# A sliding-window attention block with a token-mixing MLP on one Trainium2 core: a new head, a new order of the attention stage, and a rearranged tail

## The chip, the core and the metric

The kernel runs on one core of a Trainium2 chip. The core has five engines that run side by side and meet through semaphores: TensorE (PE, matmuls; its weight loads are shown apart as PEld), VectorE (DVE), ScalarE (ACT), GpSimd (POOL) and SyncE (SP), which here only issues DMA transfers. The metric is the device time of one execution in microseconds (us). Before the change three runs took 251.11 us (median; 250.66 to 253.0).

## The reference

`x` is 2048 tokens by 512 channels. A condition vector `c` gives six modulation rows. Then come two residual branches: attention with 32 heads of 16 channels in a causal window of 256 tokens, and an MLP that mixes tokens (its matrices act along the token axis).

```python
mod = (silu(c) @ w_mod).reshape(1, 6, 1, 512)        # sa, ca, ga, sb, cb, gb
h = layernorm(x) * (1 + ca) + sa
q, k, v = heads(h @ wqkv)
p = softmax(where(0 <= i - j < 256, q k^T / 4, -1e9))
x = x + ga * ((p v) @ wo)
h = layernorm(layernorm(x) * (1 + cb) + sb)          # the MLP has a layernorm of its own
u = gelu(h^T @ w1 + b1)                              # w1: 2048 x 1792
x = x + gb * (u @ w2 + b2)^T                         # w2: 1792 x 2048
```

## The kernel before

**Tiles.** Tokens lie in 16 tiles of 128 (`xres[t]`), in four groups of four. Heads lie in groups of eight (128 channels), so that "slice" `s` (0 to 15) is group of tokens `s // 4` and group of heads `s % 4`.

**Head** (L498 to L627, written out by hand). The four first tiles of `x`, the modulation columns for `sa` and `ca` (`wmod`, v = 0 and 1, one DMA each, L339) and `wqkv` are loaded. TensorE runs "fills", `warm(n)`, L504: matmuls on zeros whose result nobody reads. Two small matmuls (L521) spread the seeds of the window's masks, which ScalarE copies to `mask_k` and `mask_q`. `fm(v)` (L546) makes the modulation as columns with 16 one-column matmuls. `norm_x(tl)` (L570) normalises a tile on VectorE, after a reciprocal root that GpSimd takes (`rstd_of`, L438); `turn_x(tl)` (L577) transposes it on TensorE, `modulate` (L598) scales and shifts the transposed rows into `h1T[0]` on VectorE and ScalarE. TensorE's order is: fills 2, c's transpose, fills 8, mask seeds, fill 1, `fm(0)`, fills 2, tiles 0 and 2, fill 1, `fm(1)`, tiles 1 and 3, fills 2. Eight dense steps (L613) then project K and Q of slice 0 into two banks, four (L617) the Q of slice 1 ("second"). Q is padded with zeros for even and odd heads (`QP`, L620, three pieces on VectorE), K is evicted by ScalarE (L624), second by VectorE to `QR[1]` (L626). ScalarE also writes the ones in V (`ones_of`).

**Attention stage** (L630 to L1182). The work is cut into tasks: 76 score units `S0` to `S75` (four for slices 0 to 3, five for each later one), each with two exponentials `E` of 128 x 1024 on ScalarE; two products `P{s}.{par}` per slice; dense groups on TensorE (`Kk`, `Qq`, `V`, `Wo` of four steps, `B` of eight steps), where a step is one 128 x 512 matmul or its four 128 x 32 quarters, with an eviction each; transposes of normalised tiles (`T`); `turn`, `recip` and `back` on VectorE with `merge` on GpSimd for the softmax division; layer norm tasks (`st1`, `ap1`, `s2`, `p2`, `m2`, `s3`, `p3`); DMA tasks on SP (`L.`, `VLU`, `bc`, `w1.`). A unit of kind A or B writes scores with 12 or 4 matmuls and then adds the masks with 8 or 12 (L716, L706, L724); kind C has 32 and 8 (L688, L697). Scores go to `ps_s`, three buffers of two banks; a unit takes two. Everything else on TensorE shares two banks, `bk0` and `bk1`.

At build time a planner (`Order`, L128) lays these tasks into one fixed order per engine. Ranks come from the table `PLACE`, earliest starts from `START`, and `PATIENCE` says how long a score unit may be held back. `HEAD_PE` only tells the planner how many TensorE instructions the head has. `BY_POOL` lists the blocks whose second layer norm is applied by GpSimd alone. `B4` to `B13` are the MLP's first matrix over the first eight token tiles, for the ten columns blocks in `PART`; they are evicted to `part` (L1177), and can fill TensorE early.

TensorE's planned order in the places that matter (x4 is four steps):

```
S0 V0.3x4 V0.0x2 S1 V0.0x2 V0.1x2 S2 V0.1x2 V0.2x4 S3 Kk3x4 Kk1x4 Kk2x4 S4 Qq2x4 P0.0 S5 P0.1 Qq3x2 S6 ...
... S40 Wo4x4 Wo7x2 S41 Wo7x2 P8.1 S42 ...
... S74 B11x4 B4x2 S75 B4x6 P15.0 P15.1 B10x8 B13x8
```

**Tail** (L1201 on). The score buffers are released to `pu0` (four banks) and `pu1` (two), in which the MLP's first matmul collects its first six column blocks; `ps_big` (two buffers for `pa`) takes the banks `bk0` and `bk1`. `t_wo(tb)` (L1252) projects the attention output of blocks 12 to 15, `t1`, `t2`, `t3` (L1273 to L1284) are their two layer norms on VectorE with the root on GpSimd; the last result is `hb[12..15]`, applied by `t_apply` (L1268). `emit_b1_group0_sc(sc)` (L1229) is a mixing step: the matmuls of token tile `sc` into `pu0` and `pu1`, four of them for `sc` below 8 and six above. `load_rest` (L1210) starts the loads of the rest of `w1` (`w1b`) and of `w2` once block 12 is projected. Then follow the remaining columns with gelu (L1318, L1245) and the second matrix (L1344) with the output.

```python
for step in range(6):
    if step < 4:
        done = t_wo(12 + step)
        if step:
            emit_b1_group0_sc(step - 1)
        else:
            load_rest(done)
    for f, n in ((t1, step), (t2, step - 1), (t3, step - 2)):
        if 0 <= n < 4:
            f(12 + n)
for sc in range(3, NT):
    emit_b1_group0_sc(sc)
```

Of the kernel before, what the change touches and what calls it, by code (L numbers as in the profile page):

```python
# [27 lines left out]
V0.3 0 V0.0 1 V0.1 2 V0.2 3 T1.1 4 Kk3 5 V1.3 6 P1.1 7 Kk4 8 P2.0 9 P1.0 10 Qq4 11 Kk1 12 mods 13 Kk2 14 Wo0 15 Wo1  # L28
16 P4.0 17 P2.1 18 V1.0 19 Qq8 20 V1.2 21 Qq5 22 Kk6 23 P5.0 24 P3.1 25 V1.1 26 Qq2 27 Qq6 28 T2.0 29 P0.0 30 T1.0
31 P0.1 32 Qq3 33 P3.0 34 P8.1 35 Kk8 36 Wo4 37 Kk5 38 bias 39 P5.1 40 V2.0 41 P4.1 42 Wo3 43 Qq7 44 Wo2 45 T2.1 46  # L30
V2.2 47 P6.1 48 P6.0 49 Kk7 50 Kk15 51 Qq12 52 T3.1 53 T3.0 54 P9.1 55 Wo7 56 P9.0 57 P8.0 58 Wo6 59 V3.3 60 Qq9 61
V2.1 62 V2.3 63 Kk10 64 P7.1 65 P7.0 66 Wo5 67 Kk11 68 V3.0 69 P10.1 70 P10.0 71 V3.2 72 P11.0 73 B12 74 Qq13 75
V3.1 76 Kk12 77 B7 78 Kk13 79 P13.1 80 Kk14 81 P12.0 81 P11.1 82 P14.0 83 P13.0 84 B5 85 B6 86 Wo9 87 Qq15 88 Wo11
89 P12.1 90 Wo10 91 Qq14 92 P14.1 93 P15.1 94 B8 95 B9 96 B11 97 B4 98 Wo8 99 P15.0 100 B10 101 B13 102 Qq11 103
Qq10 104 Kk9 105 Wo0. 0 turn4.1 1 Qq4. 2 recip0 3 turn2.0 4 Wo1. 5 st1.1.2 6 Qq3. 7 Kk7. 8 st1.2.1 9 V2.2. 10
turn0.1 11 recip1 12 Kk2. 13 Qq7. 14 p2.2 15 mods. 16 V3.3. 17 recip3 18 T1.1. 19 Kk11. 20 V0.2. 21 recip5 22 back1
23 Kk4. 24 turn3.1 25 V1.3. 26 turn5.1 26 V2.0. 27 s2.3 28 turn1.0 29 back9 30 Kk1. 31 B12. 32 turn1.1 33 T1.0. 34
recip4 35 recip9 36 Wo2. 37 back0 38 Kk8. 39 back5 40 V1.0. 41 p2.4 42 Kk10. 43 Kk6. 44 Qq6. 45 p2.1 46 Qq12. 47
recip7 48 Kk3. 49 turn7.1 50 bias. 51 turn5.0 52 Wo3. 53 turn7.0 54 turn6.1 55 turn0.0 56 V1.1. 57 T2.1. 58 Qq2. 59
s2.1 60 Qq5. 61 V1.2. 62 V2.1. 63 s3.1 64 turn2.1 65 back2 66 V0.1. 67 back6 68 st1.1.1 69 back3 70 turn3.0 70  # L40
st1.1.3 71 st1.2.2 72 recip2 73 s3.0 74 st1.3.3 75 T2.0. 76 turn9.0 77 s2.2 78 Qq8. 79 Kk15. 80 st1.2.0 81 V0.3. 82
T3.0. 83 fold3 84 Kk5. 85 back4 86 st1.2.3 87 turn9.1 88 st1.1.0 89 Wo6. 90 fold0 91 fold2 92 fold1 93 Qq10. 94
V0.0. 95 s3.2 96 recip6 97 s2.0 98 turn6.0 99 turn4.0 100 st1.3.1 101 st1.3.0 102 back8 103 Wo5. 104 Wo7. 105 Wo4.
106 V2.3. 107 s2.6 108 s2.7 109 Kk9. 110 back7 111 T3.1. 112 s2.5 113 turn8.1 114 Qq11. 115 recip8 116 s3.3 117
turn8.0 118 s2.4 119 Qq9. 120 st1.3.2 121 Qq13. 122 s3.8 123 V3.2. 124 s3.10 125 turn14.0 126 s3.11 127 B5. 128 B6.
129 back12 130 turn15.1 131 B11. 132 recip15 133 turn13.0 134 Wo9. 135 back14 136 s2.9 137 s3.9 138 B10. 139 V3.0.
140 turn14.1 141 B13. 142 back11 143 turn12.1 144 recip14 145 turn10.1 146 recip13 147 turn15.0 148 Kk13. 149 B8.
150 turn11.1 151 Kk14. 152 turn12.0 153 s3.5 154 B7. 155 p2.6 156 p2.7 157 B4. 158 s3.4 159 V3.1. 160 recip11 161
Kk12. 162 turn10.0 163 turn13.1 164 Qq15. 165 s2.11 166 recip10 167 s2.8 168 turn11.0 169 Wo10. 170 s3.7 171 Wo11.
172 p2.9 173 recip12 174 s3.6 175 Wo8. 176 s2.10 177 back10 178 Qq14. 179 p2.11 180 back15 181 B9. 182 back13 183  # L50
r1.1 0 zeros 1 Qp4.1 2 ap1.1.2 3 Qp3.1 4 VLU0a 5 m2.0 6 q2.0 7 p2.0 8 ap1.1.3 9 merge3 10 Qp8.1 11 ap1.3.2 12 r1.2
13 Qp11.1 14 ones2 15 VLU0 16 ap1.1.0 17 Qp5.0 18 Qp7.0 19 r1.3 20 Qp1.1 21 Qp4.0 22 Qp1.0 23 Qp2.1 24 m2.2 24 p3.2
25 Qp10.0 26 merge6 27 ap1.2.0 28 Qp5.1 29 Qp12.0 30 ap1.3.1 31 ap1.3.3 32 m2.3 33 m2.1 34 ap1.2.3 35 p3.0 36 merge1
37 ap1.2.1 38 merge9 39 merge2 40 Qp3.0 41 ap1.1.1 42 Qp2.0 43 merge0 44 Qp9.0 45 Qp6.0 46 merge4 47 Qp8.0 48
ap1.3.0 49 Qp7.1 50 Qp6.1 51 ap1.2.2 52 ones1 53 Qp11.0 54 merge5 55 p3.5 56 merge8 57 Qp10.1 58 m2.4 59 p3.3 60
Qp9.1 61 merge7 62 p2.3 63 merge11 64 Qp13.0 65 merge10 66 p2.5 67 p3.8 68 q3.2 69 merge15 70 p3.9 71 p3.10 72
merge14 73 m2.5 74 m2.7 75 q2.2 76 Qp14.1 77 m2.9 78 merge13 79 p3.7 80 Qp13.1 81 m2.6 82 Qp15.1 83 p3.6 84 p2.8 85
q2.1 86 merge12 87 m2.8 88 p3.1 89 p3.11 90 m2.10 91 q3.1 92 p2.10 93 p3.4 94 Qp12.1 95 q3.0 96 Qp15.0 97 Qp14.0 98
m2.11 99 w1.7 0 VLU8 1 VLU11 2 w1.11 3 VLU14 4 VLU5 5 bc. 6 w1.10 7 L.x14 8 VLU3 9 w1.0 10 VLU13 11 w1.2 12 w1.12 13
VLU10 14 L.wo1 15 w1.5 16 w1.13 17 VLU4 18 w1.4 19 L.m2.1 20 L.m4.1 20 w1.8 21 VLU15 22 bc1 23 w1.3 24 VLU12 25 L.x8  # L60
26 L.x11 27 L.x12 28 w1.15 29 VLU2 30 L.m5.1 31 L.m4.0 32 L.m5.0 33 L.m3.1 34 VLU1 35 w1.9 36 VLU9 37 w1.14 38
L.m2.0 39 bc3 40 L.x15 41 VLU7 42 w1.6 43 L.x13 44 VLU6 45 L.x9 46 L.m3.0 47 bc0 48 bc2 49 w1.1 50 L.b1 51 L.x10 52
# [60 lines left out]
HEAD_PE = 148  # L123
# [141 lines left out]
def kernel(  # L265
# [72 lines left out]
    for v in (0, 1):  # L338
        dma.dma_start(out=wmod[:, :, v * D : (v + 1) * D], in_=w_mod_v[:, :, v * D : (v + 1) * D])  # L339
# [84 lines left out]
    def ones_of(n, a):  # L424

        nc.scalar.activation(
            out=Vring[n][:, 2 * a : 2 * a + 2, :, DH : 2 * DH],
            in_=zero[:].rearrange("p (a h d) -> p a h d", a=2, d=DH), func=ACT.Identity, scale=0.0, bias=1.0,
        )

# [7 lines left out]
    def rstd_of(var, n, name):  # L438
        ve = small.tile([P, n], DT.float32, name=name + "_ve")
        nc.gpsimd.tensor_scalar(out=ve[:], in0=var, scalar1=EPS, scalar2=0.0, op0=ALU.add, op1=ALU.add)  # L440
        r = small.tile([P, n], DT.float32, name=name)
        nc.gpsimd.tensor_tensor(out=r[:], in0=ve[:], in1=mhalf[:, 0:n], op=ALU.pow)
        return r
# [54 lines left out]
    with tc.manual_schedule():  # L498
# [19 lines left out]
        warm(8)  # L518
        rows = bank(1)
        for n in range(2):  # L520
            nc.tensor.matmul(rows[:, 0:NS], lhsT=spread[n][:], rhs=seed[n][:], start=n == 0, stop=n == 1)  # L521
# [12 lines left out]
        for odd in range(2):  # L534
            r1[0, odd] = rstd_of(mv1[0][:, odd : odd + 3 : 2, 1], 2, "r1")
        nc.scalar.activation(out=mask_k[:], in_=rows[:, 0:192], func=ACT.Copy)
        for n, c0 in ((0, MF), (1, MO)):
            nc.scalar.activation(
                out=mask_q[:, 128 * n : 128 * n + 128].rearrange("p (a b) -> p a b", a=2),
                in_=rows[:, c0 : c0 + 64].unsqueeze(1).to_broadcast([P, 2, 64]), func=ACT.Copy,  # L540
            )
        for a in range(2):
            ones_of(0, a)
        ps_fm = ps_s.tile([P, 8], DT.float32, name="pss")

        def fm(v):  # L546
            for oc in range(ND):
                col = v * ND + oc
                for k in range(ND):
# [27 lines left out]
        def turn_x(tl):  # L577
            for dc in range(ND):
                nc.tensor.transpose(place(dc, tl, tl + 1), xn1[0, tl][:, dc * P : (dc + 1) * P], identity[:])
# [37 lines left out]
        for dc in range(4):  # L617
            dense_step(second[:], wqkv[:, dc, P : 2 * P], h1T[0][:, dc, :], dc == 0, dc == 3)
# [770 lines left out]
```

## Time and profile before

| what | value |
|---|---|
| three runs | 251.11 us median (250.66, 251.11, 253.0) |
| the profiled execution | 251.63 us, of which the span from first to last instruction is 249.9 |
| TensorE busy | 240.5 us (96%) |
| VectorE, ScalarE, GpSimd busy | 168.1, 157.7, 125.2 us |
| the 152 exponentials | 140.6 us busy |
| DMA | 28.14 MB, mean 113 GB/s |

A group of the page reads: line, engine, operation, tile written and tiles read, shapes, count; then busy time, mean ns of one, and the idle time of the engine just before them with what ended it. The chain that ended last is printed as start, length, what; the timeline as start, length, engine, line, operation, and in brackets the idle time before. Matmuls overlap, so the length of a row of n matmuls is longer than n times their distance by the last one's own duration. A wait row names who waited for whom, the total, the times and the longest.

### The profile page before, as it was taken

Reading aid. Unit: us, or ns where it says so; the run is one execution under the profiler, and the core shown is the slowest. Engines: PE = TensorE matmul, PEld = TensorE weight load, DVE = VectorE, ACT = ScalarE, POOL = GpSimd, SP = SyncE. Lnnn points to the kernel's source line nnn. Section 1 sums busy time; section 2 is a strip of 40 time slices with the busy share of each in tenths; the row PEclk is TensorE's granted clock in tenths of the full one; section 3 lists DMA queues with packets and bytes.
Section 4 is the critical chain, followed back from the end, with each engine's and each line's share of the span. In section 5 each row is a group of like instructions: output and inputs, shape, how many; then the busy total and the mean of one; then the engine's idle time right before and its main releaser. Section 6 shows DMA issues by size and latency. Waiting matters only on the chain.

```text
span 249.9 us, 10602 instructions
## 1 busy us (share of the span) xinstructions
PE 240.5 (96%) x4710; PEld 126.5 (51%) x4710; DVE 168.1 (67%) x324; ACT 157.7 (63%) x183; POOL 125.2 (50%) x228
## 2 busy tenths in 40 slices
PE   8999999989999999999999999989999999999994
PEld 2644745545654555655554664544444444444443
DVE  7686879869997978787958686679824404251544
ACT  5467999999999999999999999200056300000000
POOL 5536952980299999869894997724400000000000
PEclk9999999999999999999999999999999999999999
DMA  6935554332460444211201010059999000201121
GB/s 202 325 106 152 149 140 137 108 76 77 121 201 3 97 121 114 74 34 23 42 10 37 18 22 3 3 164 390 415 410 384 6 0 5 81 28 56 42 88 42
DMA packets 25490, 28.14 MB, mean 113 GB/s; under 512 B 10212, under 2 KB 22628, under 8 KB 25444
## 3 DMA queue, kind: packets, MB, share of 16 engines
q1 hardware_dynamic: 25148, 27.20, 34.8%
q8 instruction: 37, 0.61, 1.0%
q10 hardware_dynamic: 296, 0.26, 0.3%
q14 instruction: 9, 0.07, 0.1%
HBM read 22.03 MB, written 2.10 MB: 97 GB/s over the span
## 4 chain that ended last, share of the span: by engine, by line
PE 72%; ACT 14%; DVE 5%; POOL 3%; DMA 3%; issue 2%; SPq 0%; ACTq 0%; POOLq 0%
PE py L1344 19%; ACT et L734 13%; PE bk L473 11%; PE bk L477 8%; PE pu L1234 7%; PE bk L759 6%; PE pu L1318 6%; PE pss L716 5%; PE bk L504 3%; PE pss L688 2%; PE pss L724 2%; PE pa L1255 1%; DMA VU<-V 1%; DMA x<-in_A_x_dram 1%; PE pss L697 1%
## 5 line engine op out<-in xcount | busy, mean ns | idle before, releaser
L734 ACT ACTIVATE et<-pss 128x1024 bf16<-128x1024 f32 x152 | 140.6, 1062 | 3.4 <-PE pss L724 3.3
L1344 PE MATMUL py<-guT,w2r 128*128 128x512 bf16 (+1 forms) x238 | 48.5, 367 | 0.0
L1344 PEld LDWEIGHTS <-w2r 128*128 128x128 bf16 x238 | 23.2, 98 | 25.4
L1351 DVE SCALAR_TENSOR_TENSOR o<-py,bFM,bc_gb 128x512 bf16<-128x512 f32 (+1 forms) x17 | 11.7, 717 | 30.5 <-PE py L1344 30.5
L781 POOL TENSOR_TENSOR merge<-t,zr 128x512 bf16<-128x512 f32 x16 | 17.4, 1084 | 19.4 <-DVE zr L777 19.4
L768 DVE STREAM_TRANSPOSE t<-bk 128x512 f32<-128x512 f32 x32 | 22.6, 710 | 6.6 <-PE bk L759 5.4
L716 PE MATMUL pss<-QP,KT 32*128 32x192 bf16 (+2 forms) x672 | 25.6, 236 | 0.9 <-ACT et L734 0.5
L913 POOL TENSOR_SCALAR QP<-QR,mask_par 128x512 bf16<-128x512 bf16 x30 | 21.6, 724 | 7.7 <-DVE QR L626 4.7
L716 PEld LDWEIGHTS <-KT 32*128 32x128 bf16 x672 | 13.4, 92 | 18.2 <-issue 14.0
L473 PE MATMUL bk<-h1T,wqkv 128*128 128x512 bf16 x76 | 20.4, 382 | 0.3 <-ACT h1T L602 0.3
L759 PE MATMUL bk<-et,V 128*32 128x64 bf16 (+2 forms) x704 | 19.3, 240 | 0.4 <-DVE V L933 0.3
L759 PEld LDWEIGHTS <-V 128*32 128x32 bf16 x704 | 14.7, 96 | 7.8 <-issue 4.2
L724 PE MATMUL pss<-mask_q,mask_k 32*128 32x64 bf16 (+2 forms) x496 | 18.3, 213 | 0.0
L1245 ACT ACT_TABLE_LOAD x1 | 1.3, 1283 | 26.0 <-issue 26.0
L1243 DVE TENSOR_TENSOR gelu_a<-pu,part 128x512 f32<-128x512 f32 x10 | 6.5, 687 | 11.5 <-PE pu L1318 8.7
L1124 POOL TENSOR_TENSOR h<-h,bc_sb 128x512 bf16<-128x512 bf16 x12 | 13.9, 1155 | 0.6
L1318 PE MATMUL pu<-hb,w1b 128*128 128x512 bf16 x64 | 14.0, 379 | 0.0
L724 PEld LDWEIGHTS <-mask_k 32*128 32x128 bf16 x496 | 13.3, 93 | 0.4
L933 DVE CAST V<-bk 128x512 bf16<-128x512 f32 x16 | 11.1, 691 | 3.5 <-PE bk L477 1.5
L477 PE MATMUL bk<-h1T,wqkv 128*32 128x512 bf16 x192 | 12.7, 382 | 0.0
L759 PE MATMUL bk<-et,VU 128*32 128x64 bf16 x448 | 11.8, 194 | 0.9 <-DMA VU<-V 0.9
L759 PE MATMUL bk<-et,VL 128*32 128x64 bf16 x512 | 12.2, 193 | 0.0
(138 smaller groups left out, 406.0 us busy)
## 6 DMA issues: line engine op xcount, KB each, us to landing
w2r<-in_B_w_dram SPq DMA_DIRECT2D x14, 512.0 KB, 10.2
w1a<-in_B_w_dram SPq DMA_DIRECT2D x16, 224.0 KB, 3.2
w1b<-in_B_w_dram SPq DMA_DIRECT2D x8, 448.0 KB, 7.2
wmod<-in_w_mod_dram SPq DMA_DIRECT2D x8, 256.0 KB, 3.0
out_dram<-otile SPq DMA_DIRECT2D x15, 128.0 KB, 1.7
x<-in_A_x_dram SPq DMA_DIRECT2D x14, 128.0 KB, 3.1
VL<-V SPq DMA_DIRECT2D x15, 96.0 KB, 2.8
VU<-V SPq DMA_DIRECT2D x27, 48.0 KB, 2.4
```

Of the source, the lines that this page charges most:

```text
L473: nc.tensor.matmul(out, lhsT=lhsT, rhs=rhs, start=start, stop=stop, skip_group_check=True)
L477: nc.tensor.matmul(out[cols, :], lhsT=lhsT[:, cols], rhs=rhs, start=start, stop=stop, tile_position=(0, 32 * j), skip_group_check=True,)
L716: mm(pss[j // 2][:, j % 2, c0 : c0 + nq], lhsT=keys(4 * tg + kb)[rows[j], :], rhs=QP[s][rows[j], par, q0 : q0 + nq], start=n == 0, stop=False,
L724: mm(pss[j // 2][:, j % 2, c0 : c0 + hi - lo], lhsT=mask_k[rows[j], 0:P], rhs=mask_q[rows[j], lo:hi], start=False, stop=n + 1 == len(masks ...
L734: e = nc.scalar.activation(out=et[:], in_=held.pop(("pss", u, a))[:], func=ACT.Exp, scale=SCORE_SCALE)
L759: nc.tensor.matmul(po[32 * j : 32 * j + 32, q0 : q0 + nq], lhsT=v(j), rhs=held["et", s, k, j // 2][:, j % 2, c0 : c0 + nq], start=n == 0, ...
L768: nc.vector.transpose(out=held["t2", s][:, par, :], in_=psum.pop(("po", s, par))[:])
L781: nc.gpsimd.tensor_tensor(out=m[:].rearrange("p (b a d) -> p a b d", a=2, d=DH), in0=t2v(s, 0, DH, DH), in1=held["zr", s][:].to_broadcast( ...
L913: nc.gpsimd.tensor_scalar(out=QP[s][:, par, :], in0=QR[s][:], scalar1=mask_par[:, par : par + 1], scalar2=0.0, op0=ALU.mult, op1=ALU.add,)
L1234: nc.tensor.matmul(pu[:, i, :], lhsT=w1_of(sc, fc), rhs=hb[sc][:], start=(sc == s0), stop=(sc == NT - 1),)
L1318: nc.tensor.matmul(pu[:, i, :], lhsT=w1_of(sc, fc), rhs=hb[sc][:], start=(sc == s0), stop=(sc == NT - 1),)
L1344: nc.tensor.matmul(pys[4 if lo else tl][:, lo:hi], lhsT=w2r[:, fc, tb * P : (tb + 1) * P], rhs=guT[fc][:, lo:hi], start=(fc == 0), stop=(f ...
```

## The change

The head, the order of the attention stage and the tail are changed; the computation is the same.

- Fills: 2, c's transpose, 10, `fm(0)`, mask seeds, tile 0, half of `fm(1)`, tile 2, the other half, tiles 1 and 3, fills 3. No fill stands from the ten to the last transposes. `fm` runs over k outermost; the DMA of v = 1 is cut in two halves by k, so three `wmod` issues stand ahead of `wqkv` on SP.
- The epsilon of the odd tiles' root is added by VectorE instead of GpSimd.
- The ones in the first V ring are one memset on GpSimd, behind two other memsets, instead of two ScalarE instructions.
- K of slice 0 is evicted in two pieces, columns 128 to 512 first.
- The masks of unit 0 are written ahead of its scores, right behind the eight dense steps; then come two steps of the second projection, unit 0's scores (12 matmuls), and the other two steps with the eviction to `QR[1]`.
- `PLACE`, `START`, `PATIENCE` (236.867 to 399.279), `HEAD_PE` (148 to 158) and `BY_POOL` (0, 3, 5, 8, 10 to 0, 2, 5, 10) are new, and so is each engine's order. Five dense groups of four steps more are issued as quarters. On TensorE:

```
S0 Kk1x4 S1 V0.1x4 V0.0 S2 V0.0x3 Qq2x3 S3 Qq2 V0.2x4 S4 V0.3x4 Kk2x2 S5 Kk2x2 Kk3x4 P0.0 Qq3x4 P0.1 S6 T1.0 T1.1 S7 ...
... S40 Wo4x4 P8.0 S41 Wo5x4 P8.1 S42 ...
... S73 B7x5 S74 B7x3 B13x3 S75 B13x5 P15.0 P15.1 B6x8
```

  On SP, before: `... bc1 L.x12 L.x14 bc3 L.x15 L.x13 bc0 VLU4 VLU5 bc2 w1.0 ...` (bc0 is the four DMAs of `bc_cb`), now `... bc1 L.x12 bc2 L.x14 bc3 VLU4 VLU5 L.x13 bc0 L.x15 VLU6 w1.0 ...`. On GpSimd, at the end, before: `... merge14 m2.10 q3.2 p3.8 p3.9 p3.10 merge15 p3.11`, now `... m2.11 merge14 q3.2 p3.9 p3.11 p3.10 merge15 p3.8`.
- Tail: two mixing steps stand ahead of the first of the last projections. The last apply of blocks 12 to 14 is done by ScalarE, with a shift that GpSimd makes in two small operations.

```diff
-    for v in (0, 1):
-        dma.dma_start(out=wmod[:, :, v * D : (v + 1) * D], in_=w_mod_v[:, :, v * D : (v + 1) * D])
+    for v, ks in ((0, slice(0, ND)), (1, slice(0, 2)), (1, slice(2, ND))):
+        dma.dma_start(out=wmod[:, ks, v * D : (v + 1) * D], in_=w_mod_v[:, ks, v * D : (v + 1) * D])
...
-        warm(8)
-        rows = bank(1)
...
+        warm(10)
...
-        for odd in range(2):
-            r1[0, odd] = rstd_of(mv1[0][:, odd : odd + 3 : 2, 1], 2, "r1")
+        for odd, eng in enumerate((nc.gpsimd, nc.vector)):
+            r1[0, odd] = rstd_of(mv1[0][:, odd : odd + 3 : 2, 1], 2, "r1", eng)
...
-        warm(1)
         for tl in (0, 2):
             norm_x(tl)
-        fm(0)
-        warm(2)
+        fm(0, 0, ND)
+        rows = bank(1)
...
         turn_x(0)
+        fm(1, 0, 2)
         turn_x(2)
         norm_x(1)
         xn_at = norm_x(3)
-        warm(1)
-        fm(1)
+        fm(1, 2, ND)
+        nc.vector.tensor_scalar_add(out=modFM[:, 4:8], in0=ps_fm[:, 4:8], scalar1=1.0)
         turn_x(1)
         turn_x(3)
-        warm(2)
+        warm(3)
...
+        nc.gpsimd.memset(Vring[0][:, :, :, DH : 2 * DH], 1.0)
...
-        nc.scalar.activation(out=Kring[0][:, 0, :], in_=first[1][:], func=ACT.Copy)
+        for lo, hi in ((P, 4 * P), (0, P)):
+            nc.scalar.activation(out=Kring[0][:, 0, lo:hi], in_=first[1][:, lo:hi], func=ACT.Copy)
...
+            second_steps((2, 3))
+            QR[1] = qrpool.tile([P, 4 * P], DT.bfloat16, name="QR")
+            nc.vector.tensor_copy(out=QR[1][:], in_=second[:])
...
+        add_masks([held["pss", 0, 0], held["pss", 0, 1]], MASKS["1"], True)
+        second_steps((0, 1))
...
+        def by_scalar(key):
+            return key[0] == 3 and key[1] < NT - 1
...
         def t_apply(out, src, key):
+            if by_scalar(key):
+                nc.scalar.activation(
+                    out=out, in_=src, func=ACT.Identity, bias=v[key, "shift"][:], scale=v[key, "r"][:],
+                )
+                return
...
+        for sc in range(2):
+            emit_b1_group0_sc(sc)
         for step in range(6):
             if step < 4:
                 done = t_wo(12 + step)
                 if step:
-                    emit_b1_group0_sc(step - 1)
+                    emit_b1_group0_sc(step + 1)
...
-        for sc in range(3, NT):
+        for sc in range(5, NT):
             emit_b1_group0_sc(sc)
```

More of the change, by code (lines that the diff above doesn't have):

```diff
@@ L33 @@
[L33 to L37, printed above, removed]
@@ L58 @@
[L58 to L62, printed above, removed]
@@ L71 @@
+BY_POOL = (0, 2, 5, 10)
 TUNABLE = ()
@@ L422 @@
     nc.gpsimd.memset(add_one[0:32, :], 1.0)
[L424 to L429, printed above, removed]
     ps_s = tc.alloc_tile_pool(name="ps_s", bufs=3, space=PSUM)
@@ L533, with fm @@
         stats_of(xres[3][:], mv1[0][:, 3, :])
-        for odd in range(2):
-            r1[0, odd] = rstd_of(mv1[0][:, odd : odd + 3 : 2, 1], 2, "r1")
[L536 to L543, printed above, removed]
+        for odd, eng in enumerate((nc.gpsimd, nc.vector)):
+            r1[0, odd] = rstd_of(mv1[0][:, odd : odd + 3 : 2, 1], 2, "r1", eng)
         ps_fm = ps_s.tile([P, 8], DT.float32, name="pss")
[L546 to L549, printed above, removed]
+        def fm(v, k0, k1):
+            for k in range(k0, k1):
+                for oc in range(ND):
+                    col = v * ND + oc
                     nc.tensor.matmul(
@@ L616, with second_steps @@
         second = ps_s.tile([P, 4 * P], DT.float32, name="pss")
-        for dc in range(4):
-            dense_step(second[:], wqkv[:, dc, P : 2 * P], h1T[0][:, dc, :], dc == 0, dc == 3)
+        def second_steps(steps):
+            for dc in steps:
+                dense_step(second[:], wqkv[:, dc, P : 2 * P], h1T[0][:, dc, :], dc == 0, dc == 3)
         for par, lo, hi in ((0, 192, 512), (1, 0, 512), (0, 0, 192)):
@@ L638 @@
         slots["qr"].take(1)
-        order.free["DVE"] = 1.6
+        order.free["DVE"] = 1.85
         held, psum = {}, {}
@@ L666, with add_masks @@
         }
+        def add_masks(pss, masks, first):
+            for n, ((lo, hi), c0) in enumerate(masks):
+                for j in range(4):
+                    nc.tensor.matmul(
+                        pss[j // 2][:, j % 2, c0 : c0 + hi - lo], lhsT=mask_k[rows[j], 0:P],
+                        rhs=mask_q[rows[j], lo:hi], start=first and n == 0, stop=not first and n + 1 == len(masks),
+                        tile_position=(32 * j, 0), skip_group_check=True,
+                    )
         def scores(u):
@@ L670, in scores @@
             tg, g8 = divmod(s, 4)
-            pss = [ps_s.tile([P, 2, 4 * P], DT.float32, name="pss") for a in range(2)]
+            pss = [held.get(("pss", u, a)) or ps_s.tile([P, 2, 4 * P], DT.float32, name="pss") for a in range(2)]
             held["pss", u, 0], held["pss", u, 1] = pss
@@ L721, in scores @@
                 masks = MASKS[k[2]]
[L722 to L728 removed]
+            if u:
+                add_masks(pss, masks, False)
+                return
+            second_steps((2, 3))
+            QR[1] = qrpool.tile([P, 4 * P], DT.bfloat16, name="QR")
+            nc.vector.tensor_copy(out=QR[1][:], in_=second[:])
+        held["pss", 0, 0], held["pss", 0, 1] = (ps_s.tile([P, 2, 4 * P], DT.float32, name="pss") for a in range(2))
+        add_masks([held["pss", 0, 0], held["pss", 0, 1]], MASKS["1"], True)
+        second_steps((0, 1))
         def exps(u, a):
```

119 lines of the change are left out of this document (64 added, 55 removed).

## The prediction, on record before the result

> **What bounds the kernel now.** I read the page's head and groups first, then the windows by stage, then the chain that ended last, ScalarE's timeline, and the waits.
>
> ```profile
> span 249.9 us, 10602 instructions
> PE 240.5 (96%) x4710; PEld 126.5 (51%) x4710; DVE 168.1 (67%) x324; ACT 157.7 (63%) x183; POOL 125.2 (50%) x228
> L734 ACT ACTIVATE et<-pss 128x1024 bf16<-128x1024 f32 x152 | 140.6, 1062 | 3.4 <-PE pss L724 3.3
> ```
> ```profile
> 14.90:60.00 45.10, 43.37 (x1223) 24.22 (x1225) 37.66 (x64) 42.69 (x46) 29.16 (x50) 1.00 0.44 116
> 60.00:100.00 40.00, 38.61 (x1188) 22.31 (x1187) 34.57 (x58) 39.96 (x45) 31.57 (x55) 1.00 0.40 110
> 100.00:157.00 57.00, 56.49 (x1646) 31.53 (x1636) 42.81 (x67) 56.99 (x63) 46.51 (x77) 1.00 0.13 29
> ```
>
> A window's columns are its length, then the busy time of TensorE, its weight loads, VectorE, ScalarE, GpSimd. TensorE bounds the whole: what it does before useful work, and every wait, is paid at the end. From the first exponential (14.90) to 157 ScalarE is full too; TensorE's waits there are 1.73 + 1.39 + 0.51 = 3.6 us. After 157 TensorE alone sets the pace.
>
> ```profile
> 20.32 0.33 PE pss L716 x12
> 20.76 2.82 PE bk L477 x48
> ```
> ```profile
> 24.02 0.98 PE bk L477 x16
> 25.00 0.50 PE bk L759 x40
> 25.51 0.33 PE pss L716 x12
> ```
> ```profile
> 56.26 1.40 PE bk L473 x6
> 57.66 0.33 PE pss L716 x12
> ```
> ```profile
> 133.16 0.36 PE pss L688 x32
> 133.52 0.29 PE pss L697 x8
> ```
> ```profile
> 141.04 0.80 PE bk L759 x56
> ```
> ```profile
> 17.14 5.61 ACT L734 ACTIVATE et<-pss 128x1024 bf16<-128x1024 f32 x6 [0.30 <-PE pss L724]
> 24.07 4.84 ACT L734 ACTIVATE et<-pss 128x1024 bf16<-128x1024 f32 x5 [1.32 <-PE pss L724]
> 56.36 3.78 ACT L734 ACTIVATE et<-pss 128x1024 bf16<-128x1024 f32 x4 [0.73 <-PE pss L724]
> 61.85 14.79 ACT L734 ACTIVATE et<-pss 128x1024 bf16<-128x1024 f32 x16
> ```
>
> The chain gives TensorE's prices: a score unit of kind A or B 0.44 us until the next work (20.32 to 20.76), kind C 0.65 (0.36 + 0.29); six dense steps 1.40 with the change back to scores (56.26 to 57.66), so 0.216 a step and 0.105 a change; a product 0.80, in the first four slices 0.62 (24.02 to 25.51 less four steps). ScalarE: sixteen exponentials in 14.79, less 1.06 for the last, are 0.915 apart, 1.82 for a unit's two. Six steps beside a score (0.44 + 1.40) just fill a unit. ScalarE's three large gaps are 0.30, 1.32 and 0.73 idle, and 0.1 to 0.2 more in the spacing of starts, where the overlap of two neighbours is lost too: 0.43, 1.4 and 0.9.
>
> **The change, part by part.** *Head.*
>
> ```profile
> 1.71 0.98 SPq L339 DMA_DIRECT2D wmod<-in_w_mod_dram  x2
> 2.32 3.59 PE L504 MATMUL bk<-zero 128*128 128x512 bf16 x8
> 8.46 0.74 DVE L572 TENSOR_SCALAR xn<-x,mv,r 128x512 bf16<-128x512 bf16 x2 [0.53 <-POOL r L442]
> 9.92 1.01 PE L579 MATMUL pss<-identity,xn 128*128 128x128 bf16 x8
> 10.73 0.64 PE L504 MATMUL bk<-zero 128*128 128x512 bf16 x2
> 11.67 1.89 PE L473 MATMUL bk<-h1T,wqkv 128*128 128x512 bf16 x8 [0.30 <-ACT h1T L602]
> 13.59 1.53 DVE L620 TENSOR_SCALAR QP<-bk,mask_par 128x320 bf16<-128x320 f32 x3 [1.30 <-PE bk L473]
> 14.35 0.40 PE L716 MATMUL pss<-QP,KT 32*128 32x256 bf16 x12
> 14.90 1.94 ACT L734 ACTIVATE et<-pss 128x1024 bf16<-128x1024 f32 x2 [0.92 <-PE pss L724]
> ```
>
> The last two tiles were normalised at 8.46 to 9.20, yet their transposes start at 9.92, behind a fill and a whole modulation block. Now half of that block stands ahead of tile 2's transposes, and no fill between; one small addition goes from GpSimd to VectorE, a part of the 0.53. So the eight transposes follow the normalisation: 9.2 + 8 x 0.10 (9.92 to 10.73) = 10.06 instead of 10.73. From there the dense work waits 0.94 for the modulated rows (10.73 to 11.67), so 11.0 at best; three fills, two at 0.43 and one at 0.22, hold it to 11.1. Eight steps of 0.216 end at 12.85. Then come the masks (0.11), two steps of the second projection (0.43) and two changes (0.2): scores at 13.6, just when the first piece of Q's padding is there (0.2 after the dense work, plus a third of 1.53). Before, four second steps stood there (14.35). Without masks behind them the scores release the exponential after 0.43 instead of 0.55 (14.35 to 14.90): 14.05 against 14.90, **-0.8**.
>
> At nothing I cost: the third wmod issue, 0.49 (half of 0.98) on SP ahead of wqkv and x4 to x7, covered by the dense work's start, which waits for ScalarE and not for a transfer (without that cover up to 0.49); K's eviction in two pieces, one fixed part more on ScalarE while TensorE is at the second projection; the ones for V, a memset on GpSimd, the idlest engine here (50%), wanted by the first product at 25.0.
>
> One assumption carries the head. A fill of 512 columns takes 0.44 at 2.32 (eight in 3.59) and a dense step 0.216 at 11.67 (eight in 1.89, less 0.38 for the last): the clock rose inside the pair at 10.73. The Trainium skill ("TensorE: Matmul & The Clock Gate", Part 1) says that a free-running window of 3.4 us in which TensorE is busy opens the clock; Part 4 says that transposes do not count as busy in the same way. The row disagrees with one window: fills ran from 2.32, and the clock rose 8.5 us later. By Part 4 the new head, with no fills between its transposes, could miss the window and open one window later, which would add 1.7 to the sum.
>
> *Places laid anew.* I went through TensorE's new order with the prices above. An interval from score unit to score unit is the score, its steps, products and changes; ScalarE stalls by what exceeds 1.82, after a credit of at most 0.35. Before: unit 3 carries twelve steps, 0.44 + 2.59 + 0.105 = 3.14, a stall of 1.25; all others together 1.75. After: unit 5 carries ten steps and two early products, 0.44 + 2.16 + 0.21 + 1.24 = 4.05, a stall of 2.1, and 0.25 more because the Q group in it waits until VectorE has evicted K from its bank; units 40 and 41 (a score, four Wo steps, a product, 2.21 each) give 0.4; the rest 1.75. So 4.5 against 3.0: +1.5.
>
> ```profile
> PE bk L759 <- DMA VU<-V: 0.9, 1, 0.9
> PE pa L1255 <- DVE part L1177: 0.8, 1, 0.8
> ```
> ```profile
> 48.11 2.77 SPq L1071 DMA_DIRECT2D bc_cb<-bc_all  x4
> ```
> ```profile
> 51.69 3.61 DMA VU<-V
> ```
>
> Two stalls outside these sums go. The 0.43: the second unit's score waited for the second projection's eviction, behind Q's three pieces; now Kk1's four steps end with it, leaving 0.05. The 0.9: slice 4's copy stood on SP behind the bc_cb issues and two x loads; now it is ahead of both, some 4 us sooner (2.77 and two x), so it lands before its product; late next would be slice 5's copy, issued right behind. New waits of that sort I bound by none and by two such, 1.8; I take 0.3, nearer to the seventy units that have none. So +1.5 - 0.4 - 0.9 + 0.3 = **+0.5**. In these intervals TensorE does eight B steps and two second steps more, less masks, 2.0 us, against its 3.6 of waits. One block less for GpSimd (BY_POOL) is a little more for VectorE, 42.81 busy of 57: nothing. After the last score stand five steps instead of six: **-0.1**.
>
> *Tail.*
>
> ```profile
> 158.99 3.66 PE bk L477 x64
> ```
> ```profile
> 161.55 0.70 DVE L790 STREAM_TRANSPOSE OT<-merge 128x512 bf16<-128x512 bf16 x1
> 163.42 1.89 PE L1255 MATMUL pa<-wod,OT 128*128 128x512 bf16 x8 [0.79 <-DVE part L1177]
> 181.10 0.41 DVE L1268 TENSOR_SCALAR hb<-h,ln_mv,ln 128x512 bf16<-128x512 bf16 x1 [0.76 <-POOL ln L442]
> ```
> ```profile
> L1212 SPq DMA_DIRECT2D w1b<-in_B_w_dram x8: 333/433/737, 164.5 to 168.3; - x8
> DMA to landing us min/median/max: 4.7/7.2/8.3
> ```
>
> Before, 16 B steps (3.46) follow the last product at 158.99, then a wait for the last B eviction to free the bank; the projections start 4.43 after the product. Now 8 B steps and 8 mixing matmuls, the same 3.46, stand there; the bank is free by then, and OT, ready 3.26 after the product (162.25), is just in time. The projections start at +3.5 with 8 matmuls (1.73) already done: 0.93 + 1.73 = -2.66. Against it: OT's merge finds GpSimd at a layer norm until about the same moment, and the last block loses its lead. The blocks' chain took from 163.42 to 181.5, 18.1; the last block's matmuls are now wanted at 17.7 instead of 19.4. ScalarE takes three applies from VectorE, two of them ahead of the last block (0.3 each, the 0.41 less overlap): 17.5. GpSimd's two small operations more per block are bounded by the 0.76 that a root takes. I allow 0.3 for both: **-2.35**. If the lead is overrun, TensorE waits by the excess. w1b, issued from +1.1 and landed from +5.8 to +13.2, is wanted from +8.6 to +17.7: hidden with 2.8 to spare.
>
> Sum: -0.8 + 0.5 - 0.1 - 2.35 = -2.75. The profiled execution took 251.63, so 248.9; the median of the runs is 0.5 lower, by which 248.4. I give 248.6.
>
> **The rivals.** *TensorE is full and gives the moved steps back.* If all of the 2.0 us is paid, the main phase costs +2.0 instead of +0.5: 250.1. For it: 100 to 157 has 0.5 us free. Against: the 85 us before have 3.1.
>
> *The clock rises earlier.* With ten fills at the start it could rise before the last transposes; what it saves there is bounded by the normalisation's end at 9.2 and the 0.94 behind it, 0.7: 247.9.
>
> *The clock rises late: the other side.* TensorE bounds, so every us past 10.8 at half speed costs half a us. At 14.35, where the scores stood, it is +1.8: 250.4; at 17.14, the second unit's exponentials, +3.2: 251.8, slower than before's median. It eats the whole 2.75 from 10.8 + 5.5 = 16.3 on. For it: no fill stands from about 6.6 to 10.06. Against: ten fills before, three behind.
>
> *The tail's fill is no gain*, because OT's merge comes 0.8 late behind GpSimd: 249.4, inside the forecast's own range.
>
> **How the numbers follow.** Forecast 0.57 (247.7 to 249.5), moved steps paid 0.2, early clock 0.08, late clock 0.15, a third of it past 16.3. The range 247.2 to 251.0 leaves out that third and some spread, about 0.12. One per cent, 2.5 us, is about what a measurement of this kernel can tell from no change: faster is below 248.6, where the forecast lies, so a little under two thirds of the forecast, most of the early clock and some spread of the paid steps make 0.5; the remainder, with the paid steps and the mild late clock, same 0.4; slower 0.1.
>
> **What would show it.** Right: a first exponential near 14.1; projections 3.5 after the last product, with no wait for part; a ScalarE gap of about 2.2 ahead of the seventh unit and no VU wait near 54. Wrong: half-speed matmuls past 11; ScalarE's gaps summing to much over 4; TensorE waiting for hb or OT.

## The result, and the profile after

The changed kernel is 1.2% slower: 254.51 us median (253.07 to 255.4, four runs) beside 251.19 of the kernel before on the same chip, a ratio of 1.0123 [1.0082, 1.0164] (in brackets the 95% interval). Its profiled execution took 254.1 us, with a span of 252.3. Before, these were 251.63 and 249.9, so the two profiles differ by 2.4 to 2.5 us. The forecast was 248.6.

The page of the changed kernel:

```profile
span 252.3 us, 10699 instructions
PE 236.6 (94%) x4739; PEld 124.7 (49%) x4769; DVE 169.3 (67%) x323; ACT 160.0 (63%) x185; POOL 126.5 (50%) x233
L736 ACT ACTIVATE et<-pss 128x1024 bf16<-128x1024 f32 x152 | 141.5, 1043 | 9.3 <-PE pss L660 6.2
```

TensorE is busy 3.9 us less (240.5 before) in a longer span. ScalarE's exponentials waited 9.3 us, where it was 3.4. The windows say where:

```profile
13.06:60.00 46.94, 43.59 (x1315) 24.56 (x1319) 36.36 (x63) 44.16 (x48) 29.15 (x50) 1.00 0.42 113
60.00:100.00 40.00, 35.65 (x1060) 21.14 (x1067) 32.92 (x55) 34.55 (x38) 30.83 (x54) 0.96 0.37 101
100.00:162.13 62.13, 59.58 (x1736) 32.82 (x1745) 48.63 (x73) 61.70 (x67) 46.35 (x77) 1.00 0.15 34
```

In the 40 us behind 60 ScalarE lost 5.4 (39.96 to 34.55), and the granted clock is 0.96 instead of 1.00. ScalarE's timeline of the changed kernel has the stall itself, as idle time in brackets:

```profile
13.06 9.49 ACT L736 ACTIVATE et<-pss 128x1024 bf16<-128x1024 f32 x10 [0.65 <-PE pss L714]
24.17 1.94 ACT L736 ACTIVATE et<-pss 128x1024 bf16<-128x1024 f32 x2 [1.63 <-PE bk L761]
26.65 11.45 ACT L736 ACTIVATE et<-pss 128x1024 bf16<-128x1024 f32 x12 [0.54 <-PE pss L695]
38.54 22.25 ACT L736 ACTIVATE et<-pss 128x1024 bf16<-128x1024 f32 x24 [0.44 <-PE pss L660]
64.98 1.94 ACT L736 ACTIVATE et<-pss 128x1024 bf16<-128x1024 f32 x2 [4.20 <-PE pss L660]
68.00 4.69 ACT L736 ACTIVATE et<-pss 128x1024 bf16<-128x1024 f32 x5 [1.07 <-PE pss L660]
```

1.63 and 0.54 are the heavy block that the prediction had placed ahead of the seventh unit; the first part shows ahead of the sixth, where ScalarE waits for a product (L761). 4.20 and 1.07 it had not placed. There ScalarE waits for scores; so what did TensorE wait for? Read backwards, in the timelines of TensorE, VectorE and SP's queue:

```profile
63.48 0.81 PE L465 MATMUL bk<-wod,OT 128*128 128x512 bf16 x2 [4.12 <-DVE x L1094]
```
```profile
61.94 0.69 DVE L985 BATCH_NORM_STATS2 mv<-x 128x6 f32<-128x512 bf16 x1 [5.16 <-DMA x<-in_A_x_dram]
62.55 0.33 DVE L779 RECIPROCAL zr<-t 128x32 f32<-128x32 f32 x1
62.80 0.63 DVE L1094 TENSOR_TENSOR x<-bk,x 128x512 bf16<-128x512 f32 x1
```
```profile
54.58 0.58 SPq L872 DMA_DIRECT2D x<-in_A_x_dram  x1
55.22 3.29 SPq L1073 DMA_DIRECT2D bc_cb<-bc_all  x4
58.55 1.66 SPq L872 DMA_DIRECT2D x<-in_A_x_dram  x1
```

TensorE's next Wo group needs a bank that VectorE must empty (L1094). That eviction stands third in VectorE's queue, behind the statistics of `x15` (L985), which nothing on TensorE's path needs soon, and which wait 5.16 us for the load of `x15`. SP issued that load only at 58.55, because the four `bc_cb` issues stood ahead of it. The Trainium skill ("PSUM — Partial Sum Buffer", Engine vs sequencer instructions) calls VectorE's queue a strict FIFO; these rows agree: TensorE had filled the bank and stood idle from 59.36 on, and the eviction ran at 62.80.

The wait costs more than itself. Windows on the places around it, the granted clock third from the right:

```profile
59.36:63.48 4.12, 0.00 (x1) 0.02 (x1) 1.54 (x4) 1.42 (x2) 0.52 (x1) 1.00 0.35 81
64.43:67.84 3.41, 3.41 (x47) 1.28 (x36) 2.13 (x5) 1.94 (x2) 2.11 (x8) 0.50 0.69 216
67.84:71.26 3.42, 3.42 (x128) 2.38 (x124) 3.04 (x7) 3.26 (x4) 1.99 (x3) 1.00 0.02 5
```

One us after work resumes the clock is halved, for 3.41 us: five Wo steps in that window, from 64.83 on, take 2.31, where the same five take 1.25 at full clock (in the run with the later statistics, below). All four runs of the changed kernel had a mean clock of 0.984 to 0.993.

The head and the tail went the other way. TensorE's timeline of the new head, and the chain of the new tail beside that of the kernel before:

```profile
2.32 4.33 PE L496 MATMUL bk<-zero 128*128 128x512 bf16 x10
8.60 0.71 PE L556 MATMUL pss<-identity,xn 128*128 128x128 bf16 x8
10.04 1.89 PE L465 MATMUL bk<-h1T,wqkv 128*128 128x512 bf16 x8
```
```profile
162.23 1.65 PE bk L761 x109
163.88 1.91 PE bk L469 x32
165.94 1.67 PE pu L1236 x7
167.62 1.73 PE pa L1257 x8
...
241.79 7.12 PE py L1362 x46
```
```profile
157.34 1.65 PE bk L759 x112
...
198.11 48.40 PE py L1344 x238
```

Eight transposes took 0.71 instead of 1.01 and the first exponential began at 13.06 instead of 14.90. From the last two products to the last `py` it is 86.68 (162.23 to 248.91) instead of 89.17 (157.34 to 246.51): -2.49.

So the profiles compare as: head -1.84; from the start of the first exponential to that of the last, called the main phase below, 149.07 instead of 142.06, +7.0; from there to the last products -0.3; tail -2.5. In all +2.4.

### The profile page after: what moved, and what is told of

It reads as the page before. It is cut to its first block, busy times and chain, and to the rows that moved or that the text cites. A ratio compares the mean times of both kernels' runs of the same rounds, so it can differ in the third digit from the quotient of the medians.

```text
span 252.3 us, 10699 instructions
## 1 busy us (share of the span) xinstructions
PE 236.6 (94%) x4739; PEld 124.7 (49%) x4769; DVE 169.3 (67%) x323; ACT 160.0 (63%) x185; POOL 126.5 (50%) x233
## 4 chain that ended last, share of the span: by engine, by line
PE 75%; DVE 7%; ACT 6%; POOL 3%; DMA 3%; issue 3%; SPq 2%; ACTq 1%; DVEq 0%
PE py L1362 19%; PE bk L465 13%; PE bk L469 9%; PE pu L1236 7%; PE bk L761 7%; PE pss L714 6%; PE pu L1336 5%; ACT et L736 5%; DMA x<-in_A_x_dram 3%; DVE h L1114 3%; PE pss L660 2%; PE pss L686 2%; PE pa L1257 1%; POOL h L1126 1%; SPq L1073 1%
## 5 line engine op out<-in xcount | busy, mean ns | idle before, releaser
L915 POOL TENSOR_SCALAR QP<-QR,mask_par 128x512 bf16<-128x512 bf16 x30 | 21.3, 717 | 10.9 <-DVE QR L908 6.5
L761 PE MATMUL bk<-et,V 128*32 128x64 bf16 (+2 forms) x704 | 19.3, 240 | 1.3 <-DVE V L935 0.5
L761 PEld LDWEIGHTS <-V 128*32 128x32 bf16 x704 | 14.9, 96 | 8.5 <-issue 4.8
L469 PE MATMUL bk<-h1T,wqkv 128*32 128x512 bf16 x256 | 17.1, 382 | 0.4 <-DVE h1T L1014 0.2
L465 PE MATMUL bk<-h1T,wqkv 128*128 128x512 bf16 x51 | 14.3, 380 | 0.9 <-DVE t L770 0.3
L1280 ACT ACTIVATE hb<-h,ln_sh,ln 128x512 bf16<-128x512 bf16 x3 | 2.4, 813 | 18.3 <-DVE ln_mv L440 12.2
L465 PE MATMUL bk<-wod,OT 128*128 128x512 bf16 x28 | 9.3, 426 | 4.3 <-DVE x L1094 4.1
L902 DVE CAST KT<-bk 128x512 bf16<-128x512 f32 x15 | 10.3, 687 | 3.7 <-PE bk L469 2.1
```

The source lines that it names most:

```text
L465: nc.tensor.matmul(out, lhsT=lhsT, rhs=rhs, start=start, stop=stop, skip_group_check=True)
L469: nc.tensor.matmul(out[cols, :], lhsT=lhsT[:, cols], rhs=rhs, start=start, stop=stop, tile_position=(0, 32 * j), skip_group_check=True,)
L761: nc.tensor.matmul(po[32 * j : 32 * j + 32, q0 : q0 + nq], lhsT=v(j), rhs=held["et", s, k, j // 2][:, j % 2, c0 : c0 + nq], start=n == 0, ...
L915: nc.gpsimd.tensor_scalar(out=QP[s][:, par, :], in0=QR[s][:], scalar1=mask_par[:, par : par + 1], scalar2=0.0, op0=ALU.mult, op1=ALU.add,)
```

## The experiments

Three theories. **A**: the late load of `x15` makes the loss, through the statistics in VectorE's queue. **B**, the rival of the prediction: TensorE is full, and moved work is paid wherever it stands. **C**: the loss lies in the head or the tail. The planner's order changes throughout with any rank, so most edits leave its plan as it is and only defer when a planned task is written into its engine's queue:

```diff
+LATER = {"bc0": "L.x15"}
...
-        t.emit()
+        if t.name in LATER:
+            self.kept.setdefault(LATER[t.name], []).append(t.emit)
+        else:
+            t.emit()
+            for do in self.kept.pop(t.name, []):
+                do()
```

**The load sooner.** The edit above: `bc0`'s four issues behind the load.

> The changed kernel, same planned order, but the four copies of slice 0's cos/sin table (bc0) are issued on SP behind the load of x15 instead of ahead of it. Theory A (the late load of x15 held DVE's statistics, those held the eviction of Wo0's bank behind them, and TensorE waited 4.1 us for that bank): x15's load is issued near 55.2 instead of 58.55 and lands near 58.6, TensorE's wait before the second product of Wo falls from 4.1 to under 1.2 us, the clock is not halved at 64.4, and the run comes to 249 to 250. Theory B (TensorE is full; the moved projections cost what they cost wherever they stand): the gap closes in place but ScalarE waits as long a little later, and the run stays at 253 to 254.5. Theory C (the loss is in the head or the tail): no change, 254.

249.65 us (248.93 to 251.47), 0.996 [0.9928, 0.9993] of the kernel before, which took 250.93 beside it. The profile's span is 247.4, 4.9 under the changed kernel's; by the two ratios the gain is 1.6%, some 4.1. (`bc0` spreads a modulation row, not the table that the expectation names.) VectorE's row and TensorE's:

```profile
58.39 0.69 DVE L991 BATCH_NORM_STATS2 mv<-x 128x6 f32<-128x512 bf16 x1 [1.54 <-DMA x<-in_A_x_dram]
```
```profile
59.94 0.81 PE L471 MATMUL bk<-wod,OT 128*128 128x512 bf16 x3 [0.51 <-DVE x L1100]
```

The wait is 0.51 instead of 4.12, and the clock stays at 1.00 (span's mean 1.0). A holds; C falls, since head and tail are untouched.

**The statistics later, the load as late as it was.**

```diff
+LATER = {"st1.3.3": "Wo3.", "r1.3": "Wo3."}
```

> The changed kernel, same planned order, but the last statistics of x15 on DVE (and the reciprocal root on POOL that needs them) are issued behind the eviction of Wo3's bank; the load itself stays late. Theory A: nothing on TensorE's path waits for x15 any more; the wait of 4.1 us and the half clock go, 5 to 5.7 us, and the run comes to 248.5 to 249.5, at or under the run with the sooner load. If instead the late load itself does the harm in another place (slice 15's projections), the stall moves to 70 or later and the run stays above 252. Theory B: 253 to 254.5.

249.59 us (248.87 to 252.57), 0.9959 [0.9924, 0.9994]. TensorE no longer waits before that group:

```profile
59.05 0.82 PE L471 MATMUL bk<-wod,OT 128*128 128x512 bf16 x3
```

Two edits that share nothing but the link between load and eviction give the same gain (spans 247.4 and 247.3). The load may be late, as long as its reader does not stand ahead of an eviction.

**Later still.**

```diff
+LATER = {"L.x15": "VLU6"}
```

> The changed kernel, but the load of x15 is issued behind slice 6's three copies as well, some 1.9 us later still. Theory A: TensorE waits about 6 us for Wo0's bank, the clock is halved for one window as in the changed kernel, and the execution comes to 256 to 256.5. If the half clock came from chance and not from the wait, some of it may be missing, 254.5.

257.21 us (two runs, 256.98 and 257.43), 1.0243 [1.0163, 1.0323]. VectorE's statistics, TensorE, and the clock in two windows:

```profile
64.43 0.69 DVE L991 BATCH_NORM_STATS2 mv<-x 128x6 f32<-128x512 bf16 x1 [6.16 <-DMA x<-in_A_x_dram]
65.97 1.44 PE L471 MATMUL bk<-wod,OT 128*128 128x512 bf16 x3 [5.12 <-DVE x L1100]
```
```profile
63.20:66.60 3.40, 0.63 (x2) 0.25 (x2) 2.17 (x5) 0.00 (x0) 1.06 (x1) 0.50 0.82 249
66.60:70.00 3.40, 3.40 (x27) 1.09 (x25) 1.80 (x3) 1.74 (x2) 2.44 (x9) 0.50 0.16 60
```

The wait grew by 1.0, not 1.9, since the load's reader began 2.4 behind its issue at 62.06, where it was 3.4 before (58.55 to 61.94). Taken from the reader, TensorE's wait follows one for one. With the statistics waiting 1.54, 4.63, 5.16 and 6.16 (the sooner load, the changed kernel's second and first profile, the later load) TensorE waited 0.51, 3.59, 4.12 and 5.12, always 1.03 to 1.04 less. Two windows were halved instead of one, but so they were in the second profile of the changed kernel (below), with a wait of 3.59. The main phase, 150.65, is 1.6 longer than the changed kernel's; another 1.3 of the profiled execution is a first exponential at 14.35 instead of 13.06, with the clock halved in the head from 8.6 to 12.0.

**Half as late.** Two of `bc0`'s four issues behind the load.

```diff
+            issue(range(2 if n == 0 else 4))
+            if n == 0:
+                HELD["L.x15"] = lambda: issue((2, 3))
```

> The changed kernel, but two of bc0's four copies are issued behind the load of x15 on SP, so that the load is late by half as much. Theory A (TensorE's stall is the lateness of that load and nothing else): the load lands near 60.3, TensorE waits 2.3 to 2.7 us for Wo0's bank instead of 4.1 (0.5 with all four behind), and the execution comes to 251 to 252, above 249.6 by those 2 us; if a wait of that length also halves the clock for a window, 253 to 253.5. If the wait is set by something else in that place, it stays at 4.1 or falls to 0.5 without a middle value.

Inconclusive: 250.84 and 256.27, too far apart to price half the delay. In the profiled one (250.84) TensorE had already lost time at 41 to 46; the statistics waited only 0.53 for the load, and TensorE not at all at 60. What it shows instead is the clock, in another place. The first row is TensorE's wait, the others windows:

```profile
PE bk L1052 <- DVE QR L911: 1.0, 1, 1.0
```
```profile
39.50:42.80 3.30, 1.85 (x68) 1.03 (x65) 3.18 (x7) 2.49 (x3) 1.80 (x3) 1.00 0.41 127
42.80:46.20 3.40, 3.40 (x33) 1.21 (x34) 2.26 (x5) 1.94 (x2) 2.99 (x10) 0.50 0.26 70
```

Two waits, of 1.00 and 0.45, together 1.45 of 3.3 us, were followed by a window at half clock.

**Both remedies.**

> The changed kernel with both remedies: the load of x15 ahead of bc0, and its statistics behind the eviction of Wo3's bank. Alone, the first left a stall of ScalarE of 0.55 at 59.8 and the second one of 0.74 at 66.8. If those stalls are the remainder of the same wait, both go and 0.5 is gained on 249.6: 249.0 to 249.2. If TensorE is full, so that a wait less in one place is a wait more in the next, 249.6 again.

250.92 us (249.36 to 252.41), 1.0002 [0.9965, 1.0039]. No gain over one remedy, rather a loss that the intervals do not separate. Eight of the ten runs have a mean clock of 0.986 to 0.993, about what one halved window of 3.41 us in 250 makes; the two at full clock took 249.36 and 249.57, like one remedy. The stalls of 0.55 and 0.74 went as expected, yet the main phase is 144.41 (144.10 and 144.21 with one remedy): 0.35 came ahead of S7 and 0.36 ahead of S36. That is what B expected. This profile also lost time in the head, which no edit touched:

```profile
2.32 4.29 PE L502 MATMUL bk<-zero 128*128 128x512 bf16 x10
8.32 0.55 PE L537 MATMUL pss<-sT,wmod 128*128 128x1 bf16 x16 [1.70 <-DMA wmod<-in_w_mod_dram]
```
```profile
6.33:9.75 3.42, 1.72 (x35) 1.15 (x34) 2.07 (x7) 0.47 (x3) 1.52 (x2) 1.00 1.13 329
9.75:13.16 3.41, 3.41 (x27) 1.97 (x25) 1.90 (x6) 1.43 (x4) 2.66 (x4) 0.50 1.05 309
```

TensorE waited 1.70 for the modulation weights behind the ten fills, where no other fill stands now; the clock, full from 6.33 to 9.75, was halved for the next window, and the first exponential began at 15.72.

**The new head and tail with the old order.** The places, start times and planner's costs of the kernel before:

```diff
-PATIENCE = 399.279
-BY_POOL = (0, 2, 5, 10)
+PATIENCE = 236.867
+BY_POOL = (0, 3, 5, 8, 10)
...
-HEAD_PE = 158
+HEAD_PE = 148
```

> The new head's code (ten fills, the first unit's masks first) and the new tail's code, but with the planned order of the kernel before (places, start times and the planner's costs). Theory A: the order alone loses; before's main phase with stalls of about 5 us stays, the head gives 0.8 to 1.8 and the tail 2.4, so 247 to 248. Theory B (the head's masks and fills cost as much as they give, later on): 249 to 251. Theory C: slower than 251.

249.95 us (249.11 to 251.58), 0.9962 [0.9933, 0.9992]. Less than expected of A, and what B said. Its span is 247.4, that of the new order with the sooner load. Its main phase (from 13.13 in both) takes 142.12 instead of 144.10, and then it loses that again: 0.3 up to the last products, and 1.73 for 32 more quarter matmuls behind them.

**The new tail alone.**

> The kernel before with the new tail alone: two mixing steps ahead of the last projections and slice 3's normalisations applied by ScalarE. The prediction's tail term of -2.35, and -2.50 from the last product to the end in the changed kernel, give 248.7 (248.4 to 249.1) if the tail's gain is the tail's own. If it came from the new order instead, 250.5 to 251.2.

249.67 us (249.26 to 251.31), 0.9958 [0.9932, 0.9984]: faster than before, though not as low as 248.7. Its first exponential, its fills, and its chain:

```profile
13.46 1.94 ACT L734 ACTIVATE et<-pss 128x1024 bf16<-128x1024 f32 x2 [0.93 <-PE pss L724]
```
```profile
2.32 3.30 PE L504 MATMUL bk<-zero 128*128 128x512 bf16 x8
```
```profile
155.72 1.65 PE bk L759 x112
157.37 3.63 PE bk L477 x64
161.00 1.83 PE pu L1234 x8
162.83 1.73 PE pa L1255 x8
...
195.73 48.40 PE py L1360 x238
```

From the products to the end it is 88.41 (155.72 to 244.13), -0.76 and not -2.49. The wait for `part` is gone; the other 1.73 in the changed kernel are the 32 quarter matmuls that its order had moved ahead of the products. And this kernel has the head of before to the letter, yet its eight fills took 3.30 instead of 3.59 and its first exponential began at 13.46 instead of 14.90.

**The kernel before once more.**

> The kernel before once more, for the time at which the clock rises. If that depends on when the execution starts against a fixed beat of 3.41 us, not on the kernel, it can rise near 5 to 7.4 here instead of 10.8 as in the first profile, with the first exponential near 13.4 instead of 14.90, as in the run with the new tail alone, which has the same head; the time would then be near 250. If the head's work sets it, 10.8 and 14.90 come again.

252.14 us; the clock rose at 10.9 (10.8 in the first profile) and the first exponential began at 14.90 again. That run alone would speak for the head's work as the cause. But other profiles with the same head have 13.46 (tail alone), 13.40 (copies sooner, below) and 16.64 (ScalarE's applies alone, below).

**The changed kernel once more.**

> The changed kernel once more. Theory A: x15's load lands more than 3 us after its statistics wait for it, TensorE waits 3.5 to 5 us for Wo0's bank near 60 and the clock is halved for a window behind it, as in the first profile: 253 to 255.5. If the wait was a chance of that one execution, it is absent or under 1 us here, and the time near 250.

254.28 us, TensorE's wait 3.59, the clock 0.50 from 61.4 to 68.2: the wait is no chance of one execution.

**The two halves of the tail.** Only the two mixing steps ahead (`by_scalar` returns False), and only ScalarE's applies (the mixing steps as before).

> The kernel before with two mixing steps ahead of the last projections and nothing else (VectorE keeps all applies). By the run with the whole new tail, the 64 B matmuls behind the last product give way after 3.57 us instead of 4.43 and TensorE has no wait for part: 0.86 from the last product to the end. If that 0.86 is the mixing steps' alone, it stands here too (last product to end 86.6 to 86.7, 249.7). If ScalarE's applies are needed to hold the shortened lead of the last block, TensorE waits here for hb by up to 0.9 and the end is that of the kernel before (87.4).

> The kernel before with the three applies by ScalarE and nothing else. Nothing waits for the applies in the tail of before (its only wait of TensorE there is the 0.79 for part), so the chain of the blocks gets shorter beside a full TensorE: no gain, last product to end 87.4, the time of the kernel before within 0.3. If the applies carried a part of the gain, 86.9 or less.

Mixing steps alone: 250.7 us, 0.9984 [0.9957, 1.0011]; in the trace TensorE waits for nothing in the tail, neither `part` nor `hb`, so the applies aren't needed for that. The lengths of its profile can't be set beside the others as they are, since the granted clock was 0.95 from start to end. From the products to the end it is 91.87. Scaled by stretches of equal work (50.38 beside 48.40 for the second matrix, 14.39 beside 13.91 for the mixing steps) this is an estimated 88.3 to 88.8, nearer to 88.41 than to 89.17. Applies alone: 250.55 us, 1.0008 [0.9975, 1.0042], and 89.17 from the products (159.45) to the end, to the hundredth that of the kernel before, with its wait:

```profile
PE pa L1255 <- DVE part L1177: 0.8, 1, 0.8
```

The applies by ScalarE do nothing for the time. That the mixing steps alone give the -0.76 is argued from the waits in the trace; the times don't separate it from nothing.

**The old order's own late copy.** In the kernel with the new tail alone:

```diff
+LATER = {"bc0": "VLU4"}
```

> The kernel with the new tail alone, and bc0's four copies issued on SP behind slice 4's copies instead of ahead of them. In the order before TensorE waited for slice 4's copy 0.3 to 1.6 us near 54 (ScalarE's stall at unit 20: 0.94, 0.33 and 1.58 in three profiles). If the copy behind four issues is late, as x15's load was in the changed kernel, that stall goes below 0.2 and 0.3 to 1.0 is gained: 248.8 to 249.3 beside the 249.7 of the tail alone. If TensorE is full anyway, 249.7.

249.5 us (248.61 to 250.65), 0.996 [0.9929, 0.9992], and the lowest span of all, 246.9. SP's queue:

```profile
46.64 0.66 SPq L948 DMA_DIRECT2D VL<-V  x1
47.34 1.33 SPq L950 DMA_DIRECT2D VU<-V  x1
48.77 0.59 SPq L951 DMA_DIRECT2D VU<-V  x1
49.41 3.61 SPq L1077 DMA_DIRECT2D bc_cb<-bc_all  x4
```

The stall at unit 20 is gone, and the main phase takes 141.30 (141.88 in the kernel with the tail alone). The gain of 0.6 in the profile is under what the times can tell (249.5 beside 249.67). This version has the lowest span and median; it beats both kernels, though not measurably the other remedied ones, and has neither the new head nor the new order.

## Why the prediction was wrong

*The step that failed* is in the order of the attention stage: "New waits of that sort I bound by none and by two such, 1.8; I take 0.3, nearer to the seventy units that have none." They measured 6.9: 5.0 is the main phase with the late load less that with the sooner one (149.07 - 144.10), and 1.95 are the small stalls that stay (next point). The prediction had read on SP that four `bc_cb` issues made the copy of slice 4 late, and credited the new order with 0.9 for putting that copy ahead of them. It named slice 5's copy as what is late next. But the same exchange put the load of `x15` behind them (`L.x13 bc0 L.x15`), and nothing in the sum asked who reads `x15`, and what stands behind that reader on VectorE. A wait of 0.9 was no measure for it: the copy had one reader on TensorE, this load holds a queue. With the halved clock behind it, it outweighs all that the change gains.

*What the moved steps cost.* Without that wait the main phase still takes 144.10 instead of 142.06: +2.0, not +0.5. That is the price of the first rival, TensorE full. Measured as the distance of the exponentials' starts beyond 0.904, their usual one, the items that the sum had named came as named: the heavy block 1.77 + 0.66 = 2.43 (2.35), units 40 and 41 0.50 (0.4), the wait for `VU` gone. Five small stalls, 0.20 to 0.55 and 1.95 together, stand against the 0.3, where the kernel before has one of 0.21. TensorE's busy time there is up by 1.0 and its idle time by 1.0 (139.49 busy of 144.10, 138.47 of 142.06): so the rival has the price right, and its reason, that the moved work is paid, for half of it; the other half are new waits. The argument against the rival, 3.1 us free before 100, took the sum of idle time for room; the run with both remedies shows a stall taken away that comes back elsewhere.

*The tail* came out at -2.49 for -2.35, its projections 3.6 after the products for 3.5, with no wait for `part`. But 1.73 of it is matmuls moved into a main phase that paid for them. On its own the tail gives -0.76, the price of the wait that it removes. The allowance of 0.3 for the blocks' chain was not needed: no wait for `hb` or `OT`.

*The head* was taken at -0.8, with the clock's rise at 10.8 as a property of the kernel. It is one of the execution. With the head of before the first exponential began at 13.40, 13.46, 14.90, 14.90 and 16.64 (and at 14.02 under the clock of 0.95), with the new one at 12.95 to 13.13 in six profiles and at 14.35 and 15.72 in two. With an early clock the new head is 0.33 ahead (13.13 beside 13.46, same order and tail), and the times of that pair, 249.95 and 249.67, show no gain. So of the -1.84 between the first two profiles about 1.4 (14.90 - 13.46) is the moment at which the clock rose. The bound of 0.7 for an early clock (13.35) fell 0.3 short: it let the normalisation end at 9.2, and it ended at 8.86. What the new head gives on average isn't settled by these runs.

*Luck.* With the sooner load the span is 2.5 under that of the first profile before (247.4, 249.9), much what was forecast. But 1.4 of it is again that profile's late clock; by the times that version gains 0.4%, 1.0 us. Without the late load the time would have lain inside the stated range, but with less than half of the gain that was forecast.

*Small slips in the sum.* 9.2 + 8 x 0.10 is 10.0, not 10.06, and one step less after the last score is 0.2 by its own price, not 0.1; measured it was 0.3. Neither matters here.

*The other side.* The chance of 0.1 for slower rested on a late clock. A late clock did come in two of the eight profiles of the new head, but not in the two of the changed kernel as it stands (13.06, 13.04); the way it went was not on the list. Of the signs of being wrong one came: ScalarE's gaps sum to 9.3.

## What to carry to other kernels

Before crediting a DMA that moves ahead of others on a queue, list what it moved ahead of, who reads that, and what is queued behind each reader. A reader that nobody waits for is dangerous when it stands ahead of an eviction in an in-order queue. Where one engine is 96% busy, a step moved out of one stage is a cost in another until a run shows otherwise; compare such changes by the whole span, not by the stage that got shorter.

## What the runs showed of the hardware

- A wait can take the clock with it, and it need not be long: 1.45 us of waits in 3.3 were followed by 3.4 us at half clock, 1.70 in 3.42 too; with a wait of 4.12 it was 3.41, with one of 3.59 it was 6.8. The idle share alone does not decide: in the changed kernel's first profile the stretch from 57.60 to 61.01, with TensorE busy for 1.76, was followed by one at full clock. Why is open. The Trainium skill ("TensorE: Matmul & The Clock Gate", Part 1) tells of a free-running window of about 3.4 us, and of the return to half speed after an idle one. The lengths agree with the window; the windows above were half idle, not idle.
- The moment of the first rise differs from execution to execution with one and the same head: the first exponential moved by up to 3.2 us (13.40 to 16.64). So one profile of each kernel can't price an edit of the head.
